# Linear attention and a feed-forward layer on one core: the issue order and the engine choices of the whole program set by another table

## The chip, the cores and the metric

The kernel runs on one core of a Trainium2 chip. The metric is the device time of one execution in microseconds (us), lower is better. Three runs of the kernel before took 789.76, 793.84 and 795.9 us. One further execution was recorded by the profiler; all rows below come from it.

## The reference

Linear attention over `q`, `k`, `v` of 8 batches, 8 heads, 576 positions and head width 64, followed by a feed-forward layer on the 4608 tokens that come out of it:

```python
q_s = softmax(q, axis=-1)                    # over the head width
k_s = softmax(k, axis=2)                     # over the positions
kv = einsum('bhsd,bhse->bhde', k_s, v)
x = einsum('bhsd,bhde->bhse', q_s, kv)       # -> 4608 tokens x 512
h = x @ w_in                                 # 512 x 2048
g = where(h >= 1, h, where(h <= -1, 0, (h + 1)**2 / 4))
out = g @ w_out                              # 2048 x 512
```

All is wanted in float32. `w_in` and `w_out` reach the device in float64, as two 32-bit words per number.

## The kernel before, in words

**Numbers.** A float32 product is made of two rounded parts per operand (high and low, type fp32r) and three matmuls: high by low, high by high, low by high. The high part is a copy with a cast on ScalarE (`high`, L1878), the low part a subtraction on VectorE or GpSimd (`low`, L1881). The weights are joined from their two words on the chip in the same manner (L597 to L639) and written to device memory, from which later stages fetch them (`fetch` L702, `fetch_second` L1861).

**Stages.** The tokens are worked in 9 chunks of 512. For a chunk, the attention of its batch is loaded (L1053 for the first batch, L1299 for the others; `q` tiles of a place share a ring of two buffers), the softmaxes are made, `k` and `q` are transposed (L1348, L1518; `kb`, `ta`, `tb`), TensorE forms `kv` (L1104, L1365), `kv_scaled` (L920 on ScalarE, L922 on VectorE) divides it by the softmax sums into `kvt`, and TensorE forms `x` from `ta`, `tb` and `kvt` (L944) in two PSUM banks that it borrows from earlier products. The first layer gives `h` in 16 blocks of 128 of the 2048 columns, the activation is a rectifier (L1738), a square (L1742 on ScalarE, L1744 on GpSimd) and a min of the two (`g_min`, L1748, VectorE), and the second layer adds up the outputs.

The first 3 chunks run plainly: `h` (L1583) and `o` (L1783), with `g_lo` (L1774) for the low part of an activation. The other 6 chunks run as 3 pairs. A pair's two layers use a form of matrix product with 7 products in place of 8 (P1 to P7): `two_first_layers` sums them in the PSUM banks `hA`, `hC` and `hb` (L1647), with snapshots of a bank (`sn`, L479 on ScalarE, L481 on VectorE) that are added to other banks (L1671); the second layer has the sums `oA` and `oX` (L1893), in two groups of four steps per pair, whose operands are combinations of activations (`change`, L1843). In the names, `hA_3_6` is bank hA of the pair that begins with chunk 3, in the 7th of its 8 steps of two blocks, and `g2_3_0_P7_1` the second operand of product P7 in the first group of that pair. One product is 6 matmuls of 512 columns.

**What sets the order.** The program first lists 3479 operations with their dependencies, without issuing them. Each has one engine or two ways to choose from. `Plan.settle()` then makes one global order of them from two written tables:

```python
for n in SECOND:
    self.ops[n].engine = self.ops[n].ways[1][0]
done = set()
for n in SEQUENCE:
```

`SEQUENCE` holds every operation's number once, `SECOND` those that run on the second of their two engines. The operations are emitted in that order, each into the queue of its engine, and an engine works its queue strictly in order. DMAs are all issued from SyncE (SP) in order, too: one that must wait for a buffer holds those behind it. TensorE (PE) has no second way for any operation. A ring hands its buffers to the operations that take them in the order in which they are listed, whatever the tables say.

Of the kernel before, what the change touches and what calls it, by code (L numbers as in the profile page):

```python
# [114 lines left out]
class Ring:  # L115
# [17 lines left out]
    14, 0, 1, 13, 42, 82, 41, 22, 55, 2, 3, 54, 15, 23, 4, 89, 9, 24, 5, 96, 16, 10, 43, 50, 11,  # L133
    25, 51, 17, 12, 56, 6, 18, 117, 27, 84, 83, 29, 44, 52, 85, 7, 19, 33, 30, 63, 86, 8, 20,
    53, 31, 64, 45, 26, 34, 57, 87, 21, 65, 35, 28, 58, 32, 46, 66, 124, 341, 36, 91, 47, 68,
    90, 48, 70, 59, 37, 92, 39, 49, 38, 74, 60, 40, 71, 97, 321, 61, 93, 75, 98, 67, 62, 72, 99,
    76, 94, 104, 69, 118, 73, 147, 119, 77, 100, 323, 120, 101, 134, 78, 80, 79, 135, 154, 125,
    81, 105, 121, 126, 106, 127, 122, 107, 343, 128, 136, 149, 108, 175, 129, 322, 162, 148,
    109, 137, 150, 182, 163, 110, 151, 324, 164, 111, 152, 155, 165, 112, 138, 156, 113, 205,
    166, 139, 157, 342, 115, 177, 158, 192, 167, 176, 140, 114, 178, 325, 116, 141, 159, 183,  # L140
    193, 326, 179, 212, 184, 194, 142, 180, 195, 185, 327, 168, 146, 196, 233, 328, 143, 207,
    206, 88, 330, 186, 220, 208, 169, 144, 344, 209, 187, 221, 197, 210, 170, 240, 222, 333,
    198, 172, 345, 213, 214, 329, 263, 223, 199, 215, 123, 145, 224, 200, 171, 234, 346, 347,
    216, 250, 235, 225, 251, 217, 236, 331, 252, 226, 237, 332, 174, 270, 227, 238, 253, 334,
    228, 173, 349, 242, 291, 241, 278, 348, 336, 254, 481, 243, 279, 265, 244, 204, 335, 264,
    203, 245, 351, 255, 202, 266, 350, 298, 201, 256, 271, 483, 232, 272, 267, 293, 257, 231,
    273, 268, 352, 229, 274, 258, 292, 280, 275, 360, 294, 281, 353, 308, 367, 282, 300, 354,
    309, 295, 355, 482, 299, 310, 296, 283, 301, 230, 484, 260, 302, 356, 388, 284, 337, 485,
    357, 358, 285, 501, 311, 303, 338, 286, 340, 339, 261, 359, 361, 395, 375, 312, 369, 502,
    362, 376, 313, 486, 363, 262, 390, 368, 314, 377, 364, 370, 378, 315, 365, 316, 289, 379,  # L150
    319, 389, 423, 380, 259, 391, 487, 405, 397, 396, 488, 381, 371, 406, 489, 503, 392, 287,
    398, 382, 372, 407, 504, 408, 383, 430, 418, 393, 505, 409, 506, 451, 507, 438, 394, 419,
    493, 491, 420, 439, 490, 410, 492, 440, 399, 290, 411, 424, 425, 288, 400, 386, 412, 426,
    458, 441, 509, 642, 413, 496, 427, 416, 508, 494, 428, 317, 431, 495, 318, 442, 511, 385,
    644, 510, 520, 432, 468, 443, 181, 433, 320, 512, 452, 387, 453, 434, 444, 469, 435, 454,
    445, 470, 459, 446, 384, 527, 460, 239, 414, 461, 513, 455, 471, 514, 643, 456, 497, 472,
    515, 522, 462, 548, 535, 498, 463, 499, 500, 645, 473, 536, 521, 474, 517, 537, 555, 720,
    523, 415, 529, 524, 447, 516, 475, 525, 417, 518, 421, 476, 448, 528, 662, 477, 530, 583,
    646, 297, 550, 449, 549, 647, 519, 538, 557, 663, 648, 565, 551, 539, 479, 556, 540, 531,
    450, 558, 552, 566, 422, 532, 559, 541, 567, 649, 560, 542, 478, 590, 664, 457, 543, 578,  # L160
    721, 568, 579, 553, 480, 665, 569, 611, 598, 554, 580, 570, 526, 545, 584, 571, 544, 666,
    592, 599, 572, 585, 581, 586, 600, 722, 547, 587, 573, 591, 601, 588, 593, 575, 602, 667,
    546, 594, 582, 603, 621, 650, 595, 622, 604, 623, 668, 605, 740, 624, 723, 606, 724, 574,
    759, 625, 669, 577, 652, 613, 727, 612, 726, 626, 725, 741, 653, 670, 728, 756, 651, 681,
    742, 757, 614, 576, 627, 615, 743, 760, 628, 758, 616, 607, 589, 671, 672, 800, 729, 753,
    673, 654, 608, 629, 730, 754, 674, 655, 630, 761, 731, 656, 766, 762, 732, 631, 675, 683,
    763, 676, 657, 610, 733, 636, 764, 767, 682, 637, 734, 677, 768, 744, 634, 769, 735, 765,
    679, 609, 796, 678, 632, 701, 745, 797, 248, 680, 633, 792, 635, 746, 770, 702, 737, 924,
    801, 793, 747, 779, 684, 780, 640, 781, 685, 771, 802, 795, 736, 755, 772, 153, 782, 803,
    794, 686, 658, 748, 804, 687, 638, 807, 693, 659, 773, 688, 839, 690, 783, 689, 750, 774,  # L170
    784, 738, 694, 703, 751, 833, 806, 805, 808, 660, 785, 809, 704, 840, 836, 820, 834, 691,
    810, 739, 705, 837, 811, 821, 841, 786, 749, 692, 812, 842, 752, 787, 877, 696, 776, 843,
    706, 695, 845, 846, 813, 844, 822, 879, 211, 823, 707, 920, 798, 814, 306, 847, 708, 249,
    709, 815, 848, 799, 824, 661, 925, 775, 921, 916, 711, 777, 710, 917, 849, 926, 790, 923,
# [2099 lines left out]
```

## Time and profile before

| | |
|---|---|
| median of three runs | 793.84 us |
| lowest and highest run | 789.76, 795.9 us |
| the profiled execution: span | 790.7 us |
| TensorE busy | 782.4 us (99%), 4144 matmuls |
| weight loads of TensorE (PEld) | 631.7 us (80%) |
| VectorE (DVE) | 630.8 us (80%), 1067 instructions |
| ScalarE (ACT) | 498.2 us (63%), 1002 instructions |
| GpSimd (POOL) | 382.8 us (48%), 321 instructions |
| DMA queues | 71.8% of 16 engines' time, 193 MB |

Busy is the time in which at least one instruction of the engine ran. The profiled execution has no time of its own beside the span; the span is 3.1 us below the median of the runs, and inside their spread. The granted TensorE clock is full in all 40 slices of the span, and TensorE is shown busy at 90% or more in all slices but the first, which has 80 to 90%.

### The profile page before, as it was taken

What the parts mean: (1) busy time and instruction counts of PE and PEld (TensorE: products, weight loads), DVE (VectorE), ACT (ScalarE), POOL (GpSimd) and SP (SyncE); (2) the same over time, 40 slices, a digit from 0 to 9 for tenths busy, and PEclk for the clock granted to TensorE, in tenths of its full rate; (3) what the DMA queues carried; (4) which work ended last, traced back from release to release, by engine and by line L of the source; (5) the groups of instructions that cost most, each with busy time, mean ns of one, the idle gap of its engine ahead of it and who ended that gap; (6) DMA issues with size and microseconds to landing.
All of it is one profiled execution on the core that took longest, in us unless ns stands there. A gap on an engine that the chain in (4) does not pass through costs nothing.

```text
span 790.7 us, 12342 instructions
## 1 busy us (share of the span) xinstructions
PE 782.4 (99%) x4144; PEld 631.7 (80%) x4144; DVE 630.8 (80%) x1067; ACT 498.2 (63%) x1002; POOL 382.8 (48%) x321
## 2 busy tenths in 40 slices
PE   8999999999999999999999999999999999999998
PEld 7777788878787788877878778787877888888886
DVE  7888999877877898888889998777779755765684
ACT  6888777565776666665676766544657644455452
POOL 4554546664657554275254355545540444541532
PEclk9999999999999999999999999999999999999999
DMA  8787967978896879886766768666567557656572
GB/s 325 228 314 228 327 229 280 356 236 282 256 323 213 272 252 323 264 291 226 242 236 233 256 210 283 225 208 223 190 216 258 204 182 267 196 204 225 177 251 91
DMA packets 72783, 193.79 MB, mean 245 GB/s; under 512 B 8080, under 2 KB 14480, under 8 KB 72720
## 3 DMA queue, kind: packets, MB, share of 16 engines
q1 hardware_dynamic: 72720, 193.00, 71.8%
q8 instruction: 33, 0.54, 0.3%
q14 instruction: 30, 0.25, 0.1%
HBM read 148.93 MB, written 44.04 MB: 244 GB/s over the span
## 4 chain that ended last, share of the span: by engine, by line
PE 91%; DVE 4%; ACT 2%; DMA 1%; issue 1%; POOL 0%; DVEq 0%; SPq 0%; ACTq 0%
PE hA L1647 16%; PE oA L1893 16%; PE h L1583 15%; PE o L1783 14%; PE oX L1893 12%; PE hC L1647 8%; PE hb L1647 4%; PE x L944 2%; PE kv L1365 2%; DMA xw<-in_w 1%; PE warm L2202 1%; PE oA L1905 1%; PE kv L1104 0%; DMA kt<-in_kt 0%; ACT r L1742 0%
## 5 line engine op out<-in xcount | busy, mean ns | idle before, releaser
L1647 PE MATMUL hA<-x,w 128*128 128x512 f32 x576 | 146.2, 391 | 0.6 <-DVE g L1748 0.6
L1893 PE MATMUL oA<-g_P,w_P 128*128 128x512 f32 x558 | 138.2, 391 | 0.0
L1878 ACT CAST g_P<-g 128x512 fp32r<-128x512 f32 x144 | 87.4, 619 | 70.6 <-PE oX L1893 28.9
L1647 PEld LDWEIGHTS hA<-x,w 128*128 128x128 f32 x576 | 107.5, 188 | 24.3 <-DVE g L1748 1.0
L1893 PEld LDWEIGHTS oA<-g_P,w_P 128*128 128x128 f32 x558 | 104.0, 188 | 23.9 <-issue 0.9
L1881 POOL TENSOR_TENSOR g_P<-g,g_P 128x512 fp32r<-128x512 f32 x52 | 70.5, 1359 | 102.3 <-ACT g_P L1878 77.6
L1783 PE MATMUL o<-wh,g 128*128 128x512 f32 x384 | 118.6, 390 | 0.1
L1893 PE MATMUL oX<-g_P,w_P 128*128 128x512 f32 x432 | 106.9, 390 | 0.0
L1893 PEld LDWEIGHTS oX<-g_P,w_P 128*128 128x128 f32 x432 | 80.8, 188 | 17.8 <-ACT g_P L1878 0.6
L1881 DVE TENSOR_TENSOR g_P<-g,g_P 128x512 fp32r<-128x512 f32 x92 | 70.9, 782 | 23.6 <-ACT g_P L1878 23.4
L1783 PEld LDWEIGHTS o<-wh,g 128*128 128x128 f32 x384 | 72.1, 188 | 15.2 <-DVE g L1774 0.5
L1583 PE MATMUL h<-x,w 128*128 128x512 f32 x312 | 81.0, 392 | 0.0
L1783 PE MATMUL o<-wl,g 128*128 128x512 f32 x192 | 75.7, 394 | 0.0
L1744 POOL TENSOR_TENSOR r<-r 128x512 f32<-128x512 f32 x38 | 40.6, 1073 | 68.2 <-ACT r L1738 68.2
L1647 PE MATMUL hC<-x,w 128*128 128x512 f32 x288 | 73.2, 389 | 0.0
L1583 PE MATMUL h<-x,x 128*128 128x512 f32 x264 | 69.0, 392 | 0.7 <-DVE g L1774 0.7
L1583 PEld LDWEIGHTS h<-x,w 128*128 128x128 f32 x312 | 58.0, 188 | 14.5 <-issue 1.6
L1742 ACT ACTIVATE r<-r 128x512 f32<-128x512 f32 x106 | 66.6, 631 | 1.4
L1647 PEld LDWEIGHTS hC<-x,w 128*128 128x128 f32 x288 | 54.0, 188 | 11.4 <-DVE g L1748 0.3
L1583 PEld LDWEIGHTS h<-x,x 128*128 128x128 f32 x264 | 49.2, 188 | 12.3 <-DVE g L1774 1.1
L1783 PEld LDWEIGHTS o<-wl,g 128*128 128x128 f32 x192 | 36.0, 188 | 9.6 <-issue 2.1
L1738 ACT ACTIVATE r<-h,half 128x512 f32<-128x512 f32 x48 | 32.8, 686 | 15.3 <-PE h L1583 14.8
(167 smaller groups left out, 1445.3 us busy)
## 6 DMA issues: line engine op xcount, KB each, us to landing
w_P<-v_P SPq DMA_DIRECT2D x84, 512.0 KB, 4.6
w<-s SPq DMA_DIRECT2D x48, 512.0 KB, 4.9
w<-b SPq DMA_DIRECT2D x40, 512.0 KB, 5.0
v<-in_v SPq DMA_DIRECT2D x32, 325.0 KB, 5.9
q<-in_q SPq DMA_DIRECT2D x36, 256.0 KB, 4.0
k<-in_k SPq DMA_DIRECT2D x28, 320.0 KB, 4.5
st<-in_w SPq DMA_DIRECT2D x16, 512.0 KB, 5.1
xw<-in_w SPq DMA_DIRECT2D x16, 512.0 KB, 5.7
```

Of the source, the lines that this page charges most:

```text
L944: nc.tensor.matmul(t[r][cols, :, p0:p1], kvt[rows, g % NKV, pr, :], q[pr]["tq"][rows, :, p0:p1], start=True, stop=True, tile_position=(r * ...
L1365: nc.tensor.matmul(kv[d, i, :], t[pr]["k"][:, j, d], t[pr]["v"][:, j, e * (D + 1) : (e + 1) * (D + 1)], start=(j == 0), stop=(j == KJ - 1) ...
L1583: nc.tensor.matmul(t["h"], lhs, rhs, start=(turn == 0 and i == 0), stop=(turn == NPAIR - 1 and i == 2),)
L1647: nc.tensor.matmul(banks[b]["h"], lhs, rhs, start=(begins and not kk and not m), stop=(ends and kk == 1 and m == 2), skip_group_check=True,)
L1738: nc.scalar.activation(t["r"], t["h"], AF.Relu, bias=half[:, :1], scale=0.5)
L1742: nc.scalar.activation(t["r"], t["r"], AF.Square)
L1744: nc.gpsimd.tensor_tensor(t["r"], t["r"], t["r"], ALU.mult)
L1783: nc.tensor.matmul(outs[c, j], t["g"][:, k, s], rhs, start=(begins and i == 0), stop=(closes and i == 2),)
L1878: nc.scalar.copy(t["g"][:, 0, :], tile_of(i, b))
L1881: by(engine).tensor_tensor(t["g"][:, 1, :], tile_of(i, b), f32(t["g"][:, 0, :]), ALU.subtract)
L1893: nc.tensor.matmul(banks[side, d], wr[c, group, k, i // 2][:, i % 2, w, d * P : (d + 1) * P], t["g"][:, g, :], start=(begins and w == 1), ...
L1905: nc.tensor.matmul(banks[SIDES[k], d], wr[c, group, k, i // 2][:, i % 2, w, d * P : (d + 1) * P], t["g"][:, g, :], start=False, stop=(ends ...
```

## The change

Only the numbers in `SEQUENCE` and `SECOND` change. The operations, their shapes and their dependencies are the same. 376 operations run on another engine than before: 148 go from POOL to DVE and 109 from DVE to POOL, 45 from DVE to ACT and 40 from ACT to DVE, 22 from POOL to ACT and 12 from ACT to POOL. Counted in instructions as issued, DVE goes from 1066 to 1118, ACT from 996 to 993 and POOL from 315 to 266 (a few operations, such as a copy by quarters, are four instructions). PE has the same 4144 matmuls, of its 767 operations 581 at another place of its queue, by 18 places at most; SP has the same 505 DMAs. The new tables take two more lines, so that every line of the code behind them has a number higher by 2 (L1647 becomes L1649).

```diff
 SEQUENCE = (
-    14, 0, 1, 13, 42, 82, 41, 22, 55, 2, 3, 54, 15, 23, 4, 89, 9, 24, 5, 96, 16, 10, 43, 50, 11,
...
+    0, 14, 1, 13, 42, 41, 82, 54, 55, 3, 2, 15, 4, 89, 22, 43, 333, 5, 23, 96, 56, 117, 9, 24,
...
 SECOND = (
-    7, 23, 32, 35, 73, 94, 139, 159, 167, 187, 347, 348, 380, 393, 400, 428, 499, 508, 516, 540,
...
+    7, 20, 32, 35, 64, 94, 139, 167, 180, 187, 217, 238, 365, 393, 400, 428, 443, 463, 553,
...
```

Number 0 is the load of the first `kt` tile and 14 that of the first `q` tile: the first two DMAs of SP change places.

**PE, first chunk, ahead of the last quarter of `h_0_7`.** The bank of `h_0_7` is freed by the low part of `h_0_5`'s activation, `g2_0_5`, on DVE. Before:

```order
L1583 MATMUL h_0_6_721<-x2_458,w_0_6_696 128x512 x3
L1583 MATMUL h_0_6_721<-x3_460,w_0_6_696 128x512 x3
L1583 MATMUL h_0_7_803<-x0_375,x13_771 128x512 x3
L1583 MATMUL h_0_7_803<-x1_378,x13_771 128x512 x3
L1583 MATMUL h_0_7_803<-x2_458,x13_771 128x512 x3
L1783 MATMUL o_0_1_558<-wl4_105,g2_0_4_705 128x512
```

The change:

```order
L1585 MATMUL h_0_6_736<-x1_382,w_0_6_708 128x512 x3
L1785 MATMUL o_0_3_575<-wl4_105,g2_0_4_698 128x512
L1785 MATMUL o_0_3_575<-wh4_104,g2_0_4_698 128x512 x2
L1585 MATMUL h_0_6_736<-x2_463,w_0_6_708 128x512 x3
L1585 MATMUL h_0_6_736<-x3_471,w_0_6_708 128x512 x3
L1585 MATMUL h_0_7_807<-x0_379,x13_768 128x512 x3
```

In both, `h_0_7` follows the end of `h_0_6`. Its first row comes at the 94th place of the queue before and at the 96th now; counted in products of three matmuls, one more stands ahead of it. On DVE `g2_0_5` goes from the 91st place to the 89th.

**PE, second group of blocks of the first pair, ahead of `x_5_1`.** `x_5_1` takes two banks: one is freed by the second scaling of `kv_6_1` into `kvt`, the other by `g_3_12`, the activation made of `hb_3_6`. Before, from the first product of `hA_3_6` (first row of each product; the row behind the last is `x`):

```order
L1647 MATMUL hA_3_6_4672<-x0_2805,w_3_6_0_4509 128x512 x3
...
L1893 MATMUL oA0_3_0_3973<-g2_3_0_P7_0_4584,w2_3_0_P7_0_4493 128x512 x2
...
L1647 MATMUL hA_3_6_4672<-x8_3415,w_3_6_1_4566 128x512 x3
...
L1893 MATMUL oA0_3_0_3973<-g2_3_0_P7_1_4603,w2_3_0_P7_0_4493 128x512 x2
...
L1647 MATMUL hC_3_6_4736<-x6_3068,w_3_6_1_4566 128x512 x3
...
L1893 MATMUL oA0_3_0_3973<-g2_3_0_P7_2_4632,w2_3_0_P7_1_4638 128x512 x2
...
L1647 MATMUL hC_3_6_4736<-x4_3103,w_3_6_2_4634 128x512 x3
...
L1647 MATMUL hA_3_6_4672<-x10_3505,w_3_6_2_4634 128x512 x3
...
L1893 MATMUL oX0_3_0_4542<-g2_3_0_P3_0_4743,w2_3_0_P3_0_4630 128x512 x2
...
L1893 MATMUL oA0_3_0_3973<-g2_3_0_P7_3_4716,w2_3_0_P7_1_4638 128x512 x2
...
L944 MATMUL x_5_1_0_4825<-ta_5_2_4238,kvt_94 64x4x80
```

The change:

```order
L1649 MATMUL hA_3_6_4673<-x0_2908,w_3_6_0_4541 128x512 x3
...
L1895 MATMUL oX0_3_0_4591<-g2_3_0_P5_3_4619,w2_3_0_P5_1_4476 128x512 x2
...
L1895 MATMUL oA0_3_0_3937<-g2_3_0_P7_0_4668,w2_3_0_P7_0_4537 128x512 x2
...
L1895 MATMUL oA0_3_0_3937<-g2_3_0_P7_1_4701,w2_3_0_P7_0_4537 128x512 x2
...
L1649 MATMUL hC_3_6_4728<-x6_3194,w_3_6_1_4666 128x512 x3
...
L1649 MATMUL hA_3_6_4673<-x8_3387,w_3_6_1_4666 128x512 x3
...
L1649 MATMUL hC_3_6_4728<-x4_3188,w_3_6_2_4695 128x512 x3
...
L946 MATMUL x_5_1_0_4776<-ta_5_2_4316,kvt_94 64x4x80
```

Ten products stood between the start of `hA_3_6` and `x_5_1`; now there are seven. ACT in the same stretch, before:

```order
L1738 ACTIVATE r_3_12_4747<-hb_3_6_4642,half_93 128x512
L479 COPY sn_P5_3_6_4758<-hC_3_6_4736 128x512
L479 COPY sn_P1_3_6_4697<-hA_3_6_4672 128x512
L479 COPY acc220_3_4777<-oX0_3_0_4542 128x512
L1878 CAST g2_3_0_P3_1_4782<-c22_3_1_3907 128x512
```

The change:

```order
L1740 ACTIVATE r_3_12_4726<-hb_3_6_4628,half_93 128x512
L481 COPY acc221_3_4737<-oX1_3_0_4592 128x512
L922 ACTIVATE kvt_94<-kv_6_1_4562,rz_6_1_4609 128x64
L481 COPY sn_P5_3_6_4753<-hC_3_6_4728 128x512
L1880 CAST g2_3_0_P7_3_4756<-g_4_6_4259 128x512
L1744 ACTIVATE r_3_12_4726<-r_3_12_4726 128x512
L481 COPY sn_P1_3_6_4697<-hA_3_6_4673 128x512
```

The scaling of `kv_6_1` was on DVE, 3 rows behind `g_3_12`; now it is on ACT. The square of `r_3_12` was on POOL; now it is the sixth of these rows on ACT, behind the snapshot `sn_P5_3_6` of `hC_3_6`.

**SP and DVE, end of the first pair's first group.** `w2_3_1_P2_0` and `w2_3_1_P1_1` are weights of the second group, `q_8_0` a load of the last batch, whose buffer is that of `q_7_0` and comes free with its transpose `ta_7_0`. SP before:

```order
L1861 DMA w2_3_1_P1_0_4933<-v1_P1_151 128x1024
L1299 DMA v_7_1_4938<-in_v 128x650
L1861 DMA w2_3_1_P1_1_4992<-v1_P1_151 128x1024
L702 DMA w_5_0_0_4996<-b0_112 128x1024
L1861 DMA w2_3_1_P2_0_5027<-v1_P2_152 128x1024
...
L1861 DMA w2_3_1_P5_0_5246<-v1_P5_154 128x1024
L1299 DMA q_8_0_5251<-in_q 128x512
```

The change:

```order
L1863 DMA w2_3_1_P1_0_4930<-v1_P1_151 128x1024
L704 DMA w_5_0_0_4959<-b0_112 128x1024
...
L1301 DMA v_7_1_4964<-in_v 128x650
L1301 DMA q_8_0_5000<-in_q 128x512
L1863 DMA w2_3_1_P2_0_5033<-v1_P2_152 128x1024
L1863 DMA w2_3_1_P1_1_5037<-v1_P1_151 128x1024
L1226 DMA xc_5_1_5085<-xk5_2_162 128x512
```

`q_8_0` stood 13 DMAs behind `w2_3_1_P2_0`; now it stands directly ahead of it and of `w2_3_1_P1_1`. DVE around `ta_7_0`, before:

```order
L1881 TENSOR_TENSOR g2_3_1_P2_2_5135<-g_3_13_4925,g2_3_1_P2_2_5135 128x512
L1881 TENSOR_TENSOR g2_3_1_P1_3_5138<-g_3_14_5018,g2_3_1_P1_3_5138 128x512
L1493 TENSOR_TENSOR q_7_0_4682<-q_7_0_4682,qzb_7_0_4968 128x512
L1518 STREAM_TRANSPOSE tb_7_1_5176<-q_7_1_4729 128x512
L1518 STREAM_TRANSPOSE ta_7_0_5180<-q_7_0_4682 128x512
L1843 TENSOR_TENSOR g_3_11_4714<-g_3_11_4714,g_3_10_4601 128x512
```

The change:

```order
L1673 TENSOR_TENSOR hb_3_7_4937<-hb_3_7_4937,sn_P1_3_7_4900 128x512
L1495 TENSOR_TENSOR q_7_1_4699<-q_7_1_4699,qzb_7_0_4948 128x512
L1495 TENSOR_TENSOR q_7_0_4684<-q_7_0_4684,qzb_7_0_4948 128x512
L1520 STREAM_TRANSPOSE ta_7_0_4993<-q_7_0_4684 128x512
L1883 TENSOR_TENSOR g2_3_1_P1_0_4995<-g_3_8_4392,g2_3_1_P1_0_4995 128x512
L483 COPY sn_P5_3_7_5002<-hC_3_7_4977 128x512
L1951 TENSOR_TENSOR acc120_3_4626<-oX0_3_0_4591,acc120_3_4626 128x512
L1883 TENSOR_TENSOR g2_3_1_P1_1_5011<-g_3_10_4600,g2_3_1_P1_1_5011 128x512
```

`ta_7_0` moved to a place three rows behind the sum `hb_3_7`, and the snapshot `sn_P5_3_7`, which was on ACT, stands on DVE two rows behind it. That snapshot must have read `hC_3_7` before TensorE adds the next product to that bank.

## Rows read from the trace of the kernel before

**Rows 1.** The page: busy us, share, instructions of each engine.

```profile
PE 782.4 (99%) x4144; PEld 631.7 (80%) x4144; DVE 630.8 (80%) x1067; ACT 498.2 (63%) x1002; POOL 382.8 (48%) x321
```

**Rows 2.** Waits of PE: line, engine waited for, us, times, longest.

```profile
PE warm L2202 <- POOL ident masks.py:199: 1.4, 1, 1.4
PE x L944 <- DVE kvt L922: 1.1, 1, 1.1
PE ep L1083 <- ACT kt L1078: 0.8, 1, 0.8
PE h L1583 <- DVE g L1774: 0.7, 1, 0.7
PE hA L1647 <- DVE g L1748: 0.6, 1, 0.6
```

**Rows 3.** Timeline, 426 to 452: start, us, engine, line, operation, out<-in, count.

```profile
428.19 2.88 PE L1893 MATMUL oA<-g_P,w_P 128*128 128x512 f32 x12
```

**Rows 4.** Timeline, the end; [idle before, and what ended it].

```profile
787.04 0.75 DVE L1985 TENSOR_TENSOR acc<-oA,acc 128x256 f32<-128x256 f32 x2 [0.76 <-PE oA L1905]
```

**Rows 5.** Timeline, the start.

```profile
1.18 0.42 SPq L1053 DMA_DIRECT2D kt<-in_kt  x1
...
6.38 1.11 PE L1083 MATMUL ep<-ident,kt 128*128 128x128 f32 x4 [0.81 <-ACT kt L1078]
...
17.23 2.04 POOL L1127 TENSOR_TENSOR q<-q,qz 128x512 f32<-128x512 f32 x2 [2.69 <-DVE k L481]
...
19.33 0.42 PEld L1143 LDWEIGHTS tp<-ident,q 128*128 128x128 f32 x4 [0.23 <-POOL q L1127]
```

**Rows 6.** Timeline, 53 to 56.5, PE.

```profile
52.79 1.52 PE L1583 MATMUL h<-x,w 128*128 128x512 f32 x6
...
55.02 1.66 PE L1583 MATMUL h<-x,x 128*128 128x512 f32 x6 [0.71 <-DVE g L1774]
```

**Rows 7.** Timeline, 408 to 417.5, PE and the scaling of kv_6_1.

```profile
408.57 1.52 PE L1893 MATMUL oA<-g_P,w_P 128*128 128x512 f32 x6
...
410.79 0.27 DVE L922 TENSOR_SCALAR kvt<-kv,rz 128x64 f32<-128x64 f32 x1
...
411.21 0.49 PE L944 MATMUL x<-ta,kvt 64*64 64x320 f32 x2 [1.12 <-DVE kvt L922]
...
413.73 1.52 PE L1647 MATMUL hA<-x,w 128*128 128x512 f32 x6
...
415.81 1.66 PE L1647 MATMUL hA<-x,w 128*128 128x512 f32 x6 [0.55 <-DVE g L1748]
```

**Rows 8.** Timeline, 395 to 411.3: product into hC_3_6 and its snapshot.

```profile
401.77 1.52 PE L1647 MATMUL hC<-x,w 128*128 128x512 f32 x6
...
403.33 0.59 ACT L479 COPY sn_P<-hC 128x512 f32<-128x512 f32 x1 [0.15 <-PE hC L1647]
```

**Rows 9.** The page, costliest groups: busy, mean ns | idle before, and its end.

```profile
L1878 ACT CAST g_P<-g 128x512 fp32r<-128x512 f32 x144 | 87.4, 619 | 70.6 <-PE oX L1893 28.9
...
L1881 POOL TENSOR_TENSOR g_P<-g,g_P 128x512 fp32r<-128x512 f32 x52 | 70.5, 1359 | 102.3 <-ACT g_P L1878 77.6
...
L1881 DVE TENSOR_TENSOR g_P<-g,g_P 128x512 fp32r<-128x512 f32 x92 | 70.9, 782 | 23.6 <-ACT g_P L1878 23.4
```

**Rows 10.** Windows: us, busy PE PEld DVE ACT POOL, PEclk, DMA share, GB/s.

```profile
100.00:120.00 20.00, 20.00 (x90) 16.56 (x89) 19.27 (x35) 14.88 (x32) 9.65 (x9) 1.00 0.68 235
620.00:640.00 20.00, 20.00 (x90) 16.57 (x89) 12.97 (x20) 9.32 (x16) 6.91 (x6) 1.00 0.66 224
```

**Rows 11.** The page, DMA issues: KB each, median us to landing.

```profile
w_P<-v_P SPq DMA_DIRECT2D x84, 512.0 KB, 4.6
```

**Rows 12.** Timeline, 426 to 452: use of the second group's weights, transpose, load.

```profile
438.95 2.88 PE L1893 MATMUL oX<-g_P,w_P 128*128 128x512 f32 x12
...
444.31 0.66 DVE L1518 STREAM_TRANSPOSE ta<-q 128x512 f32<-128x512 f32 x1
...
450.63 0.85 SPq L1299 DMA_DIRECT2D q<-in_q  x2
```

492 rows, old and new, of tables (SECOND, SEQUENCE) are left out of this document.

## Prediction

> **What bounds the kernel now.** I read the page first: TensorE is busy 782.4 of 790.7 us, while VectorE, the next, is at 80% [rows 1]. Then the waits of TensorE, because only there can another order win anything: five are over half a microsecond, and two of them are at the start [rows 2]. Then the timeline around each. TensorE's busy time is taken up step by step: twelve matmuls of 512 columns in a row last 2.88 us and six 1.52 [rows 3, 7], so each further one costs 1.36 / 6 = 0.227 us and a product of six 1.36 us. The work of TensorE is the same 4144 matmuls after the change, so its 782 us stay. The rest of the span is 8.3 us: 1.4 before the first matmul, 0.8 for `ep`, 2.4 in the three later waits [rows 2], and 790.7 − 787.0 = 3.7 after the last matmul, whose result VectorE takes up at 787.04 [rows 4].
>
> **The start.** `kt` now goes ahead of the first `q`. The `ep` transpose waited 0.8 us for the exponential of `kt` [rows 5], so the most it can gain is 0.8. But a chain behind it has no room: POOL's scaling of the last two `q` ends at 17.23 + 2.04 = 19.27, and the transposes that use it start at 19.33, 0.06 later [rows 5]; an earlier `ep` doesn't move that chain, unless its loads move too. I take −0.3, with 0 and −0.8 as ends.
>
> **The three waits.** The wait as printed is idle time; the delay is start minus the end of the step ahead.
> - `h_0_7`: the step ahead began at 52.79 and takes 1.36, `h_0_7` began at 55.02 [rows 6]: 0.87 lost. The change puts one more product of three matmuls ahead of it, 0.68, and moves `g2_0_5` two places up on VectorE: −0.7 to −0.87, I take −0.8.
> - `x_5_1`: 408.57 + 1.36 to 411.21, 1.28 lost behind the scaling of `kv_6_1` on VectorE, which ended at 411.06 [rows 7]. In the change that scaling is early on ScalarE, and `g_3_12` decides. Take T as the start of `hA_3_6`. Seven products put `x_5_1` at T + 9.5. The product into `hC_3_6` is the fifth, so it starts at T + 5.44; before, one that began at 401.77 had its snapshot begun at 403.33, 1.56 later, 0.59 long [rows 8]. ScalarE then has the snapshot (T + 7.0 to 7.6), a cast and the square, about 0.62 each [rows 9], to T + 8.8; `g_3_12` on VectorE, at most 0.78 [rows 9], is done at T + 9.6. That is where `x_5_1` arrives: the wait goes, but nothing is left in hand. −1.2, with 0 (VectorE held up by as much) and −1.28 as ends.
> - `hA_3_7`: 413.73 + 1.36 to 415.81, 0.72 lost for `g_4_12` [rows 7]. In the change `hA_3_7` follows `x` (1.16 with its switch: 411.21 to 413.73, less one product) and three more products, near T + 14.8; the sum into `hC_3_6` can start when its seventh product is done, T + 9.7, and an addition, rectifier, cast, square and min of at most 0.78 each end by T + 13.6. −0.7, ends 0 and −0.72.
>
> Together −2.7, at most −2.87.
>
> **Moved work.** 148 + 40 operations come to VectorE and 109 + 45 leave it, 34 more; by 0.782 each [rows 9] that is 27 us, so VectorE is busy about 658 of 790 us, 83%. POOL gives up 49 operations of about 1.36, some 66 us, and ScalarE takes 15 more of 0.62, 9 us [rows 9]. None of that is on the path by itself: what hides it is TensorE's full queue. Where the cover is thin it costs: from 100 to 120 us VectorE is already busy 19.27 of 20 us, while from 620 to 640 it has 7 us free [rows 10]. So I cost the moves at nothing as a sum, and price the places where VectorE is now late as new waits.
>
> One such place can be worked out. In the change, 33 rows of VectorE lead from `g_3_12` to the snapshot `sn_P5_3_7`, and `hC_3_7`'s next product, which must not overwrite it, stands 17 products and `x` behind `x_5_1`: 17 × 1.36 + 1.16 = 24.3 us. By the mean of all VectorE instructions, 630.8 / 1067 = 0.59 [rows 1], the 33 rows, 36 instructions with a copy by quarters, take 21.3 us, by 0.782 each 25.8 [rows 9]: from 3.0 in hand to 1.5 late. All three old waits were for VectorE, and it gets more work, so I take new waits of 1.0 in all, one or two of the size of the old ones; the ends are 0 and 5.8, twice what the old three cost. Below 0 can't be, since 1.4 + 0.8 + 2.4 + 3.7 is already all of the 8.3 us.
>
> The tail: the last operations of TensorE are the same; 0, with 3.7 staying.
>
> **Sum.** 790.7 − 0.3 − 2.7 + 1.0 = 788.7 for a profiled execution. That execution's span is 3.1 below the median of the runs (its time outside the span isn't shown), so **791.8 us** as a median, 0.3% faster; I call that no change, since less than 1% (7.9 us, below 785.9 or above 801.8) is what runs that spread from 789.8 to 795.9 can't tell apart.
>
> **Rivals.**
> - *Old waits give way to new ones of the same sum.* For it: VectorE at 83%, `x_5_1` without anything in hand, 24.3 us against 21.3 to 25.8. Against: the three long waits are each answered by a visible move. Span 790.7, time 793.8.
> - *All waits go.* 790.7 − 0.8 − 2.87 = 787.0, time 790.1. For it: order changes on TensorE are by 18 places at most, each of a size that a few matmuls give. Against: the two thin places above. Even this is under 1%.
> - *SP is held.* `q_8_0` waits for `ta_7_0`, and the weights of P2 and P1 stand right behind it. Before, that transpose ended at 444.31 + 0.66 = 445.0 and the load went out at 450.63, harming nobody; the first product of P2 began at 438.95 [rows 12]. In the change those products come about where they did. A weight load takes 4.6 us to land [rows 11] and two issues ahead of it some 0.7: if the transpose still ended at 445.0, P2 would start at 450.3 and TensorE would be 450.3 − 438.95 = 11.4 us behind where it was, whatever was won ahead of it: 802.1, time 805.2. The point from which it decides: `ta_7_0` ending later than 438.95 − 5.3 − 2.0 (0.3 + 2.7 − 1.0, what TensorE wins ahead of it) = 431.7. By the order it stands two rows of VectorE ahead of the thin snapshot above, and that snapshot is due four products and `x`, 6.6 us, ahead of P2: at 438.95 − 2.0 − 6.6 = 430.4, so `ta_7_0` ends near 428.8, 2.9 in time, if VectorE is.
> - *TensorE isn't the bound at all.* TensorE at 99% counts matmuls that overlap; weight loads are only 80% busy [rows 1]. In a stretch without a wait the loads are at 16.57 of 20 us, 83% [rows 10], for the same 90 matmuls in a stretch with a crowded and one with an idle VectorE, so 83% is what a full queue looks like. Were the gap free time, the next engine would decide, VectorE at 658, time 661. The Trainium skill, "Perfetto Trace Analysis", section "Identifying the Most-Contended Engine", says that matmul busy time is a bad measure and weight-load busy time a good one; by that rule alone 20% would be open, and the two windows here speak against it.
> - *The tables do nothing that the queues feel:* 793.8, as the first.
>
> **Chances.** Forecast 0.45; same sum 0.25; all waits gone 0.15; SP held 0.10; TensorE not the bound 0.02; nothing felt 0.03. By the ends of its terms the forecast itself spans 790.1 (787.0 + 3.1) to 799.6 (790.7 + 5.8 + 3.1), most of it the new waits. The range 786 to 798 takes in the first three cases with the spread of a median of few runs, and leaves SP held, TensorE not the bound and the forecast's worst end outside; 786 and not 790 at the low end because single runs were up to 4.1 below their own median. Faster by over 1% needs more than every wait there is, 0.07 with an odd median and the fourth rival; slower by over 1% is SP held and a like mishap, 0.11; within 1% 0.82.
>
> **What would show it.** In the profile after: TensorE busy within 2 us of 782 with x4144; VectorE near 658, POOL near 317. Waits of TensorE: `h` for `g`, `x` for `kvt` and `hA` for `g` gone or under 0.3, `ep` below 0.8; in their place one or two new ones on VectorE, of half to one microsecond, first `hC` for a snapshot `sn` on VectorE near 430, or `x` for `g` near 407. If `oX` near 438 waits for a DMA, SP was held. The granted clock stays at 1.00, as it did through all waits here [rows 10]. I am wrong if the waits' sum after the start is over 4 us, or if a wait of several microseconds stands where none was.

## The result and the profile after

The changed kernel takes **801.42 us** in the median of six runs (797.97 to 806.74), the kernel before 793.82 in six beside it (789.76 to 795.9): a ratio of 1.0102 [1.007, 1.0135]. A second set of six gave 1.0107 [1.0083, 1.0132]. I had predicted 791.8, 786 to 798. The change is 1% slower, and the prediction has the wrong sign.

The profiled execution of the change took 802.27 us with a span of 800.5, 9.8 more than the span before. The list of runs shows 1.8 us outside the span, where I had put 3.1 between span and median: the execution profiled before took about 792.5, 1.3 below the median.

The page, as [rows 1, 9, 11], with the busy us, share and count of each engine first:

```profile
PE 784.8 (98%) x4144; PEld 632.4 (79%) x4144; DVE 637.5 (80%) x1119; ACT 504.2 (63%) x999; POOL 320.3 (40%) x272
...
L1883 DVE TENSOR_TENSOR g_P<-g,g_P 128x512 fp32r<-128x512 f32 x102 | 73.2, 725 | 22.6 <-ACT g_P L1880 22.3
...
w_P<-v_P SPq DMA_DIRECT2D x84, 512.0 KB, 5.0
```

TensorE is still the bound, with 2.4 us more busy time; the other 7.4 us of the 9.8 are idle time (790.7 − 782.4 = 8.3 before, 800.5 − 784.8 = 15.7 now). VectorE got 52 instructions more and only 6.7 us more busy time. A weight load of the second layer takes 5.0 us to land, in the median, in place of 4.6. The waits of TensorE, as [rows 2] (us, times, longest):

```profile
PE hA L1649 <- DMA w<-b: 3.6, 1, 3.6
PE h L1585 <- DVE g L1776: 2.9, 2, 1.7
...
PE ep L1085 <- ACT kt L1080: 1.1, 1, 1.1
PE oA L1895 <- DMA w_P<-v_P: 1.0, 1, 1.0
PE hC L1649 <- DMA w<-s: 0.7, 1, 0.7
PE tp L1145 <- POOL q L1129: 0.5, 1, 0.5
PE et L1088 <- DVE tb L483: 0.5, 1, 0.5
PE o L1785 <- DVE g L1776: 0.2, 1, 0.2
```

The three waits of before are gone. In their place stand three for DMAs (5.3 us), where there were none, and three for VectorE (3.1). Both signs by which I had said I would be wrong have come: the waits after the start add up to 8.4 us, over 4, and one of 3.6 stands where none was. To see where each microsecond was lost, I compared the start times of matmuls in the two traces at equal amounts of matmul work. The lag of the change behind before goes in steps:

| place (us of the span) | step | what stands there |
|---|---|---|
| start, to 20 | +0.9 | `q` and its transposes |
| 52 to 57 | −0.6 | the old wait of `h_0_7`, gone |
| 92 | +1.1 | `h` waits for `g` on VectorE |
| 182 | +2.0 | `h` waits for `g` on VectorE |
| 255 to 300 | +0.7 | no single wait |
| 302 to 321 | +6.1 | `hA` waits for a weight load (4.5), then a lower clock (1.6) |
| 353 | +0.9 | `oA` waits for a weight load |
| 414 | +0.8 | `hC` waits for a weight load |
| 412 to 420 | −1.5 to −2.0 | the old waits of `x_5_1` and `hA_3_7`, gone |
| 470 to 500 | −0.55 | small ones |
| end | +9.8 | (steps read at points: they add up to within 0.5) |

**The largest step.** The timeline of the change from 296 to 316 (start, us, engine, line, operation):

```profile
296.84 0.62 ACT L782 CAST w_s<-ss 128x512 fp32r<-128x512 f32 x1
...
299.26 0.69 DVE L1457 TENSOR_REDUCE qa<-q 128x16 f32<-128x512 f32 x1 [1.82 <-DMA q<-in_q]
...
301.06 0.68 DVE L786 TENSOR_TENSOR w_s<-ss,w_s 128x512 fp32r<-128x512 f32 x1
...
301.77 0.32 SPq L830 DMA_DIRECT2D s<-w_s  x1
...
306.06 0.32 SPq L704 DMA_DIRECT2D w<-b  x1
...
313.49 1.99 PE L1649 MATMUL hA<-x,w 128*128 128x512 f32 x6 [3.61 <-DMA w<-b]
```

and the chain of waits there:

```profile
301.77 4.23 DMA s<-w_s
...
306.06 7.38 DMA w<-b
```

`w_s` is a combination of weights; its low part goes to device memory (`s<-w_s`), and a later load (`w<-b`) must wait for that store. Before, POOL made the low part 0.07 us after its cast. Now it is on VectorE behind two reductions that wait for a load of `q`: 3.6 us after the cast ended. The store takes 4.23 to land, the load then 7.38. Before, the load was issued 4.0 us ahead of its matmul:

```profile
299.96 0.32 SPq L702 DMA_DIRECT2D w<-b  x1
...
303.94 1.55 PE L1647 MATMUL hA<-x,w 128*128 128x512 f32 x6
```

In that trace it had landed at 303.72: 0.22 us ahead of its use ("in hand" below), in a profile in which TensorE waits for no DMA at all. That landing of 3.8 us was a quick one. In runs 11, 12 and 15 below, which keep before's loads up to here, the same load takes 5.1 to 6.0, and `hA` waits 0.4 to 1.1 for it; so up to 1.1 of the 6.1 is the luck of the one execution that I predicted from. The windows after the wait (us, busy PE PEld DVE ACT POOL, PEclk, DMA share, GB/s):

```profile
314.00:318.00 4.00, 4.00 (x12) 3.10 (x12) 1.94 (x4) 0.59 (x1) 0.00 (x0) 0.58 0.04 16
318.00:322.00 4.00, 4.00 (x19) 3.32 (x18) 1.83 (x3) 3.84 (x10) 1.69 (x2) 1.00 0.51 134
```

After 3.61 us of idle TensorE, the granted clock is 0.58 for four microseconds, so mostly at the lower of its two levels: 12 matmuls where the next four have 19.

**The step at 182.** The change's timeline from 175 to 185:

```profile
178.79 1.35 DVE L483 COPY kh<-ka 64x8 f32<-64x8 f32 x2
178.82 1.30 POOL L786 TENSOR_TENSOR w_s<-ss,w_s 128x512 fp32r<-128x512 f32 x1 [3.09 <-ACT w_s L782]
...
180.08 1.29 POOL L850 TENSOR_TENSOR vw<-wh,wl 128x512 f32<-128x512 f32 x1
180.18 1.74 DVE L786 TENSOR_TENSOR w_s<-ss,w_s 128x512 fp32r<-128x512 f32 x1
...
183.32 0.68 DVE L1776 TENSOR_TENSOR g<-h,g 128x512 fp32r<-128x512 f32 x1
...
184.05 1.19 PE L1585 MATMUL h<-x,w 128*128 128x512 f32 x4 [1.72 <-DVE g L1776]
```

Two copies of 64x8 take 1.35 us and a subtraction 1.74, each while POOL runs an instruction of 1.3. The activation's low part `g`, for which TensorE waits, stands behind them. In both traces VectorE's instructions last longer beside POOL when all their inputs are in SBUF: the low parts (L1881 before) 0.68 alone, and 1.00 in the mean where POOL runs beside them for over 0.1 us; in the change 0.69 and 0.88. Those with an input in PSUM, the transposes and the reductions last the same. The Trainium skill, "SBUF — State Buffer", section "SBUF: two separate sides", says that VectorE and GpSimd share a pair of ports which one instruction holds to its end, so that the other "fully blocks"; these rows agree.

### The profile page after: what moved, and what is told of

Same layout as the page of the kernel before. It is cut to its first block, busy times and chain, and to the rows that moved or that the text cites. A ratio compares the mean times of both kernels' runs of the same rounds, so it can differ in the third digit from the quotient of the medians.

```text
span 800.5 us, 12278 instructions
## 1 busy us (share of the span) xinstructions
PE 784.8 (98%) x4144; PEld 632.4 (79%) x4144; DVE 637.5 (80%) x1119; ACT 504.2 (63%) x999; POOL 320.3 (40%) x272
## 4 chain that ended last, share of the span: by engine, by line
PE 82%; DVE 6%; DMA 6%; ACT 3%; issue 1%; POOL 0%; SPq 0%; DVEq 0%; ACTq 0%
PE oA L1895 15%; PE hA L1649 15%; PE h L1585 12%; PE oX L1895 12%; PE o L1785 11%; PE hC L1649 8%; PE hb L1649 4%; PE x L946 2%; PE kv L1367 2%; DMA w<-s 1%; DMA w<-b 1%; DMA w_P<-v_P 1%; DMA st<-in_w 1%; DVE g L1776 1%; ACT sg L606 1%
## 5 line engine op out<-in xcount | busy, mean ns | idle before, releaser
L1649 PE MATMUL hA<-x,w 128*128 128x512 f32 x576 | 145.3, 391 | 3.6 <-DMA w<-b 3.6
L1649 PEld LDWEIGHTS hA<-x,w 128*128 128x128 f32 x576 | 107.7, 188 | 26.9 <-DMA w<-b 4.0
L1883 POOL TENSOR_TENSOR g_P<-g,g_P 128x512 fp32r<-128x512 f32 x42 | 54.9, 1311 | 142.4 <-ACT g_P L1880 126.4
L1883 DVE TENSOR_TENSOR g_P<-g,g_P 128x512 fp32r<-128x512 f32 x102 | 73.2, 725 | 22.6 <-ACT g_P L1880 22.3
L1649 PE MATMUL hC<-x,w 128*128 128x512 f32 x288 | 73.3, 390 | 0.7 <-DMA w<-s 0.7
L1744 ACT ACTIVATE r<-r 128x512 f32<-128x512 f32 x116 | 72.6, 630 | 1.6
L1649 PEld LDWEIGHTS hC<-x,w 128*128 128x128 f32 x288 | 53.9, 188 | 12.3 <-ACT r L1744 1.1
L1746 POOL TENSOR_TENSOR r<-r 128x512 f32<-128x512 f32 x28 | 31.0, 1112 | 64.9 <-ACT r L1740 61.5
L1341 POOL TENSOR_TENSOR k<-k,kc 128x640 f32<-128x640 f32 x19 | 25.5, 1345 | 49.7 <-DVE kc L1333 46.9
```

The lines of the kernel that those rows point to most:

```text
L1341: by(engine).tensor_tensor(k, k, at, ALU.subtract)
L1649: nc.tensor.matmul(banks[b]["h"], lhs, rhs, start=(begins and not kk and not m), stop=(ends and kk == 1 and m == 2), skip_group_check=True,)
L1744: nc.scalar.activation(t["r"], t["r"], AF.Square)
L1746: nc.gpsimd.tensor_tensor(t["r"], t["r"], t["r"], ALU.mult)
L1883: by(engine).tensor_tensor(t["g"][:, 1, :], tile_of(i, b), f32(t["g"][:, 0, :]), ALU.subtract)
```

## The experiments

Experiments write their tables in the lines of the table before, so their line numbers are those of before (L1583, L1647). The diffs are schematic: numbers are operations. Ratios are to the kernel before, run beside it.

**1 and 2: which part of the program loses.** The change's first 1056 operations (to 200 us of TensorE) and then before's order, and the reverse with before's first 1077:

```diff
-SEQUENCE = after
+SEQUENCE = after[:1056] + [n for n in before if n not in after[:1056]]
```

> The order and the engines of the change for all that it issues up to the point where TensorE is at 200 us, the rest in the order and on the engines of before. Theory L (most of the loss is loads that reach their use with too little lead, the worst at 309 us of the changed kernel) expects what stands ahead of 200 us in the two profiles: TensorE is 3.7 us later there (0.9 at the start, 1.1 at 92, 2.0 at 182, minus 0.6 at 55), so 3 to 4.5 us over before, 797 to 798. Theory V (it is VectorE and POOL, wherever they are crowded) expects the same here. A theory that the loss is spread evenly over the program expects a quarter of 8, 2 us.

> The reverse: before up to 200 us, the change's order and engines behind it. By the two profiles TensorE loses 6.0 more us after 200 (6.1 around 309, 0.9 at 353, 0.9 at 414, minus 2.0 for the two old waits near 412 and 0.5 later): 4 to 7 us over before, 798 to 801, if theory L is right, since the thin loads are all behind 200 us; and a wait of several us of hA for a load near 305. If the wait at 309 was an accident of one execution, it is 0 to 1 us over before.

Measured: 799.93 us, 1.0084 [1.0069, 1.01], and 803.38, 1.0129 [1.0092, 1.0167]. The first keeps the steps of the change's beginning (+0.8 and, at 182, +2.0), the second lacks them; but both lose at the joint near 210, 3.8 and 5 to 7 us, where loads and casts that one order had done are still to do in the other. So a splice adds its own waits, and the halves can't be added up. What the two runs show is that the loss is in more than one place.

**3 and 4: the queue of SP alone.** SP's DMAs in before's order with all else from the change, and the reverse:

```diff
-SP's operations at their places in after
+SP's operations at the places, counted in TensorE's operations, that they have in before
```

> The changed kernel with its DMAs (all of SP's queue) put back to where they stood among TensorE's operations before, as far as their inputs allow; TensorE, VectorE, ScalarE and POOL keep the order and the engines of the change. Theory L expects the waits of TensorE for DMA (3.6, 1.0 and 0.7 us) to go and the leads of the weight loads to come back (about 20 of 196 under 3 us, where the change has 55): 5 to 7 us below the changed kernel, 794 to 796. Theory V expects no gain, 800 to 802.

> The kernel before with only SP's queue changed: each DMA where the change puts it among TensorE's operations, as far as its inputs allow; all engines' order and choices as before. Theory L expects thin leads (40 or more of 196 weight loads under 3 us) and waits of TensorE for DMA of 2 to 6 us in sum, 796 to 800. Theory V expects 793 to 795.

Measured: 842.01, 1.0621 [1.0586, 1.0655], and 847.12, 1.0668 [1.064, 1.0696]. Both are far off what I expected. TensorE's waits are then mostly for VectorE and ScalarE, which wait 64 and 67 us for DMAs (6.5 before, 28.6 in the change): in each table the order of the loads is fitted to the order of the engines, and breaking that fit costs some 50 us. That doesn't decide between the theories; it says that no queue can be judged by itself.

**5: fewer of POOL's instructions beside VectorE.** The three operations of POOL at 92 and 182 to VectorE:

```diff
 SECOND = (
+    525, 1083, 1091,
```

> The changed kernel with three operations put from POOL to VectorE, in the same order: the weight subtraction that POOL begins at 91.0 us, and the two at 178.8 and 180.1. Theory V (in the two new waits of h for g, at 92 and 182 us, VectorE is held while POOL runs on the same SBUF operands: a conversion takes 1.45 in place of 0.42, a small copy 1.35 in place of 0.33, a subtraction 1.74 in place of 0.68) expects the two waits to shrink although VectorE gets three more subtractions of 0.68: the wait at 182 from 1.7 to about 1.0, and the three long VectorE instructions to be gone; the time 0 to 1.5 below the changed kernel. The rival (VectorE simply has too much to do there) expects both waits 0.7 to 1.4 longer, and the time 1 to 2 above.

Measured: 800.74, 1.0092 [1.0075, 1.0109]. Its timeline from 176 to 190:

```profile
177.38 0.35 DVE L481 COPY kh<-ka 64x8 f32<-64x8 f32 x2
...
177.75 0.69 DVE L784 TENSOR_TENSOR w_s<-ss,w_s 128x512 fp32r<-128x512 f32 x1
...
179.24 0.68 DVE L784 TENSOR_TENSOR w_s<-ss,w_s 128x512 fp32r<-128x512 f32 x1
179.84 1.29 DVE L848 TENSOR_TENSOR vw<-wh,wl 128x512 f32<-128x512 f32 x2
...
181.04 0.68 DVE L1774 TENSOR_TENSOR g<-h,g 128x512 fp32r<-128x512 f32 x1
...
181.78 1.65 PE L1583 MATMUL h<-x,w 128*128 128x512 f32 x6 [0.63 <-DVE g L1774]
```

VectorE has two instructions more there, and is done sooner: the copies take 0.35 in place of 1.35, `w_s` 0.68 in place of 1.74, and the wait is 0.63 in place of 1.72. The steps fall from 1.1 to under 0.1 and from 2.0 to 0.9. At 182 POOL's hold on VectorE is the cause; at 92 the step comes and goes in the change itself, and run 13 shows when. The total hardly shows it: the loads further on still come late (`hA` waits 3.0 us).

**6 to 8: repairing the loads by hand.** Number 6 puts the one low part of the largest step back on POOL, right behind its cast; 7 moves 37 weight loads that had under 3 us in hand up by 1 to 18 places in SP's queue (its diff is such moves alone); 8 does both and lists operation 476 ahead of 529 and 978 ahead of 1086.

```diff
 SECOND = (
-    1560,
 SEQUENCE = (
-    1658, ..., 1560, ..., 1561,
+    1560, 1561, 1658, ...,
```

> The changed kernel with one operation given back to POOL, the low part of the last sum of first-layer weights (on VectorE it stands behind two reductions that wait for a q load until 299 us), and with the store that needs it ahead of one load in SP's queue. The store's landing is what the weight load of hA at 309 us waits for before it may be issued. Theory L: that load goes out about 1.5 to 3 us earlier, the wait of hA for DMA falls from 3.6 to 0 to 1.5 us, and TensorE's clock isn't lowered behind it: 3 to 6 us below the changed kernel, 795.5 to 798.5. If the long wait was the accident of a slow landing (7.4 us), the wait stays or is gone without any of this and the time is within 1 us of 801.4.

> The changed kernel with only 37 of SP's 505 DMAs moved up in its queue, by 1 to 18 places: weight loads whose room was free over 1 us before they were issued and that landed under 3 us ahead of use. Theory L expects the waits of TensorE for DMA behind 330 us (1.0 and 0.7) to go and the loads with under 3 us in hand to fall from 55 of 196 to 25 or fewer, while the wait at 309, which isn't among them, stays: 1 to 2.5 us below the changed kernel, 799 to 800.5, and runs that spread less than its 798 to 807. Theory V expects 801 to 802.

> The changed kernel with all of it: the operation given back to POOL with its store ahead, the 37 loads up, and the low part of g ahead of the conversion at 92 us and ahead of the subtraction at 180 us in VectorE's queue. If the steps by which TensorE falls behind in the changed kernel are additive, 6.1 at 309, 0.9 at 353, 0.9 at 414, 1.1 at 92 and 2.0 at 182 go, 11 of them in all, and it comes out at 790 to 793, level with before or up to 0.5% faster (the three old waits of before are then gone too). If the changed order only trades one wait for another, 796 or more.

Measured: 802.26, 1.0119 [1.01, 1.0138]; 804.88, 1.0139 [1.0116, 1.0161]; 801.08, 1.0107 [1.0087, 1.0127]. None is better than the change. In 6 the wait for the load is gone, and another of the same size stands at the same place (waits from 290 to 314):

```profile
ACT x L1251 <- DMA xc<-xk: 4.8, 1, 4.8
...
PE o L1783 <- ACT g L1771: 3.6, 1, 3.6
```

By the chain, that load of `xc` takes 8.27 us to land. In 7 the wait near 309 stays, as I had expected, since its load isn't one of the 37; SP issues the same DMAs around it, and it takes 8.25 us to land. The waits at 353 and 414 are gone, also as expected, but one of 1.6 stands at 622, and the time is no better:

```profile
PE hA L1647 <- DMA w<-b: 4.5, 1, 4.5
...
PE oA L1893 <- DMA w_P<-v_P: 1.6, 1, 1.6
```

The weight loads that land under 3 us ahead of TensorE's first use fall from 55 to 22 in 7, which is what I had asked of it, and to 20 in 8; before it was 18. Neither is faster than the change. So the loss isn't one late operation, and it isn't in the number of thin weight loads either: near 309 whichever load is waited for lands late, and with the weights moved up VectorE and ScalarE still wait 30.8 us (7) and 40.9 us (8) for DMAs.

**9 and 10: half the bytes.** The 196 weight loads (112 for the first layer, 84 for the second) each fetch half. These kernels leave out the low parts of the fetched weights; the high part stands in their place:

```diff
-nc.sync.dma_start(f32(ws_tile(name)[:, :n]), src[:, part])
+nc.sync.dma_start(f32(ws_tile(name, 1)[:, :n]), src[:, part, :1])
...
-nc.sync.dma_start(f32(w2_tile(name)), second[group, k][:, part])
+nc.sync.dma_start(f32(w2_tile(name)), second[group, k][:, part, :1])
```

> The kernel before with every fetched weight block (196 loads of 512 KB) loaded by half, the high part alone, which then stands for the low part too: 50 MB of 194 MB less to move, every other operation, order and engine as before. All theories expect no more than 1 us of difference to before, 792.5 to 794.5, since before shows hardly a wait for DMA on TensorE's path. It is the yardstick for the next run.

> The changed kernel with the same 196 loads by half. Theory L, in the form that it has by now (the change's order lets DMAs arrive just in time or late, for VectorE and ScalarE as much as for TensorE: 33.9 us of waits for DMA on these engines against 6.5 before, in the same places where TensorE falls behind) expects most of the loss to go with the traffic: 791 to 795, at most 1.5 above the same kernel of before, and the waits for DMA down to under 15 us. Theory V (VectorE and POOL, whatever the loads do) expects 798 to 801, as without.

Measured: before 791.11, 0.9999 [0.9986, 1.0012]; the change 795.26, 1.0045 [1.0028, 1.0063]. The page and the waits of TensorE of the change with half loads:

```profile
w_P<-v_P SPq DMA_DIRECT2D x84, 256.0 KB, 3.2
```

```profile
PE h L1583 <- DVE g L1774: 3.7, 4, 2.0
PE warm L2202 <- POOL ident masks.py:199: 1.4, 1, 1.4
PE ep L1083 <- ACT kt L1078: 1.2, 1, 1.2
PE tp L1143 <- POOL q L1127: 0.9, 1, 0.9
PE et L1086 <- DVE tb L481: 0.5, 1, 0.5
PE x L944 <- DVE kvt L922: 0.2, 1, 0.2
```

Loads that land in 3.2 us in place of 5.0 give the kernel before nothing and the change 0.6 of its 1.0 to 1.07 points. No wait of TensorE for a DMA is left, and no step at 302 to 353; the steps at 92 (+1.2) and 182 (+2.2) stay, as do the gains (−2.0 at 410, −0.55 at 500). This tells the two causes apart. It doesn't take away all that I had expected of it: the change is still 4.15 us above its yardstick, where I had said at most 1.5, and TensorE, VectorE and ScalarE still wait 20.4 us for DMAs, where I had said under 15 (33.9 with whole loads, 6.5 before).

**11 and 12: the gains by themselves.** The kernel before, with only the moves that free the old waits: numbers 1940 and 2088 (both waits near 412), and in the first of the two also 230 (that of `h_0_7`).

```diff
 SEQUENCE = (
-    308, ..., 230, ..., 2095, ..., 1940, ..., 1943, ..., 2088,
+    230, 308, ..., 1940, 2095, ..., 2088, 1943, ...,
```

> The kernel before with three operations moved by one place each: one product of the second layer ahead of h_0_7 at 55 us, one product of P3 ahead of x_5_1 at 410 us, and g_4_12 ahead of one low part in VectorE's queue at 413 us. No DMA moves and no engine changes. If the three old waits are each ended by what the prediction named, TensorE gains 0.7, 1.3 and 0.7 us: 790.5 to 791.5, ratio 0.9965. If the waits move on to the next operation, 793 to 794.

> The kernel before with only the two moves at 410 us: the product of P3 ahead of x_5_1, and g_4_12 ahead of the low part in VectorE's queue; nothing moves ahead of 400 us. With all three moves TensorE had won 2.0 us there, and lost what it had won at 55 us and more to kv's transposes and to a weight load at 305 us. If gains stay where no thin load lies behind them: 2.0 us, 790 to 792 or a ratio of 0.9975. If any gain here is taken back later: 0.9995 or more.

Measured: 791.55, 0.9995 [0.9981, 1.0009], and 792.48, 1.0005 [0.9991, 1.002]. No gain that can be told from none, and both intervals leave out the ratios that I had expected, 0.9965 and 0.9975. With all three, 2.0 us are won at 412 to 419, and waits that were not there before take 1.4 and 1.1:

```profile
PE kv L1365 <- DVE st L612: 1.4, 1, 1.4
PE hA L1647 <- DMA w<-b: 1.1, 1, 1.1
```

The wait of `hA` isn't the moves' alone: it is 0.5 in 12 and 0.4 in 15, where nothing is moved ahead of it. With the two, 1.6 us are won and given back by 430.

**13: the change once more.**

> The changed kernel once more, to see which of its steps come back in another execution. Theory L expects the total again near 801, the wait of hA or of what stands next to it at 300 to 310 us again, of a size that differs by 1 us or more, and the steps at 182 and 353 us again within 0.5. If the long wait at 309 was an accident, this profile shows none of it and a time under 797.

Measured: 799.12, 1.0107 [1.0083, 1.0132]. Its waits for loads are other ones:

```profile
PE h L1585 <- DVE g L1776: 1.7, 1, 1.7
...
PE x L946 <- DVE kvt L924: 1.1, 1, 1.1
PE hC L1649 <- DMA w<-s: 1.0, 1, 1.0
...
PE hA L1649 <- DMA w<-b: 0.6, 1, 0.6
```

The 3.6 us at 309 are 0.6 here, and the clock stays at 1.00 through 305 to 320; the step at 182 is +2.0 again, those of 258 to 328 add up to +4.0, and the end is at +6.0. The step at 92 is absent. There the change's first trace has (from 88 to 96)

```profile
91.00 1.31 POOL L641 TENSOR_TENSOR w<-xw,w 128x512 fp32r<-128x512 f32 x1
91.15 1.45 DVE L611 TENSOR_SCALAR st<-st 128x512 uint32<-128x512 uint32 x1
```

and this one (from 87 to 95)

```profile
90.28 0.40 DVE L611 TENSOR_SCALAR st<-st 128x512 uint32<-128x512 uint32 x1
90.36 1.49 POOL L641 TENSOR_TENSOR w<-xw,w 128x512 fp32r<-128x512 f32 x1
```

Where POOL began 0.15 us ahead, VectorE's conversion took 1.45; where VectorE began 0.08 ahead, it took 0.40. The largest row of one profile is one throw of the dice; what lasts is the step at 182, and that the loads have little in hand (54 of 196 under 3 us again).

**14: both causes taken away.** Half loads and the three operations of number 5.

```diff
 SECOND = (
+    525, 1083, 1091,
...
+nc.sync.dma_start(f32(ws_tile(name, 1)[:, :n]), src[:, part, :1])
```

> The changed kernel with loads by half (795.3, 0.45% over before) and with the same three operations put from POOL to VectorE as in an earlier run. If what is left of the loss with loads by half is the holding of VectorE by POOL at 92 and 182 us, the steps there fall from 1.2 and 2.2 us to 0.3 and 1.1, and the time to 793 to 794, 0.2% over before. If VectorE is just too busy, the steps grow by 0.7 and 1.4 and the time to 797.

Measured: 794.12, 1.0018 [1.0009, 1.0027]. That is another 0.27 points off 1.0045, with intervals that only just part. In its profile the step at 92 is +0.3, as expected, and the one at 182 +1.6, where I had expected 1.1. 0.18 points, some 1.4 us, are left.

**15: before first, then the change.** The first 1988 of the 3479 operations in before's order, the others in the change's, so that the thin stretch from 90 to 353 is left out and the gains at 412 are kept.

```diff
-SEQUENCE = after
+SEQUENCE = before[:1988] + [n for n in after if n not in before[:1988]]
```

> Before's order and engines up to its operation 1988 of 3479, somewhat ahead of 400 us, where the two orders have issued all but four of the same operations; the change's order and engines behind it. All profiles of the changed kernel show TensorE winning 2.0 us around 410 and 0.5 at 470, and losing nothing over 0.5 behind 400 but for loads that come late. If the gain at 410 needs the change's order behind it (taken alone it was given back within 20 us), and the joint costs nothing: ratio 0.997, 790. If the change's thin loads behind 400 us or the joint cost as much: 1.000.

Measured: 796.47, 1.0038 [1.0018, 1.0058]. The joint at 392 costs about 3.4 us (2.5 of it in one wait of `hb` for `g`); the gains from 412 to 500 are there, 1.7 to 2.5, and 1.4 more is lost at 606 to 612. No order that I ran beats the kernel before.

## Why the prediction was wrong, step by step

- **TensorE is the bound:** right. It is x4144 and busy 784.8, a little over my 782 ± 2, since one stretch ran at the lower clock. The weight loads are busy only 79%, and still the waits of TensorE lengthen the time, so that share is no measure of free time here.
- **The three waits, −2.7:** right, by the working, in the change's trace: −0.6 at 55 (−0.8), and −1.5 to −2.0 for the other two (−1.9). In the change's timeline from 416 to 426 neither `x` nor `hA` has an idle time ahead of it, against 1.12 and 0.55 [rows 7]:

```profile
416.98 0.77 PE L946 MATMUL x<-ta,kvt 64*64 64x320 f32 x2
...
421.15 4.24 PE L1649 MATMUL hA<-x,w 128*128 128x512 f32 x18
```

- **SP held by `q_8_0`:** right that it wasn't: `oX` waits for no DMA, and the snapshot `sn_P5_3_7` held nobody.
- **The start, −0.3:** wrong sign, +0.9. `ep` did start earlier, but the chain that I had named as the one without room came 0.9 later [rows 5]:

```profile
17.74 0.25 DVE L1197 RECIPROCAL qz<-qz 128x16 f32<-128x16 f32 x1
...
18.13 2.05 POOL L1129 TENSOR_TENSOR q<-q,qz 128x512 f32<-128x512 f32 x2 [3.57 <-DVE k L483]
```

  I had taken that chain as unmoved, while VectorE's order ahead of it changed. The step is larger than this pair of traces shows. The scaling ends at 17.7 to 19.3 us in the six traces that begin in before's order (before, 2, 9, 11, 12, 15), of which the one that I predicted from is the latest, and at 19.6 to 20.7 in the nine that begin in the change's (the change, 1, 5 to 8, 10, 13, 14): 1.6 later in the mean.
- **The new waits, +1.0 with ends 0 and 5.8:** the step that failed. They came to about 11.6 us in the profile, twice the upper end, of which 7.8 at loads (1.6 of it the lower clock behind the longest wait), 3.1 at VectorE beside POOL, and 0.7 that I can't place. I looked for places where VectorE is late, and put the loads at nothing without a reason, but for one place, around `q_8_0`. Had I put every weight load's landing beside TensorE's first use of it, I would have seen a danger: of the 196, 4 landed under 1 us ahead of that use before, and 12 in the change; under 3 us, 18 and 55. From issue to first use the 10th percentile fell from 8.5 to 6.7 us for first-layer loads and from 7.9 to 6.3 for second-layer ones, against landings of weights that reach 8.3 us. The second figures are from the trace after, but the places of SP's loads against TensorE's products were in the two orders before the run, for all 196 and not only for the two behind `q_8_0`. This count is a sign and not the cause: run 7 brought it back to 22 and was no faster. What halving the bytes shows is that the time loads take to land carries most of the loss; which loads, those of weights or those of `q`, `k` and `xc` for which VectorE and ScalarE wait, no run took apart.
- **VectorE's load, 658 us:** 637.5. I priced 34 operations more at 0.782 each. With POOL's busy time down by 62.5 us, VectorE is held less: its low parts take 0.725 in the mean and not 0.782, and what all its instructions last beyond the median of their form falls from 42.1 to 28.5 us in sum. So the mean got better while two places, where POOL and VectorE meet ahead of a `g` that TensorE needs, got worse by 3.1 us.
- **The clock stays at 1.00:** wrong in the profiled execution, where the fall cost 1.6 us; right in the one of run 13.
- **Rival "old waits give way to new ones of the same sum":** the nearest. New waits did take the place of the old, but it looked for them at VectorE alone, which has 3.1 of the 11.6 us, and its size is wrong by a factor of four.

What is shown: the bytes of the loads carry 0.6 of the 1.0 to 1.07 points (9 and 10), POOL's three instructions about 0.27 with the loads out of the way (14 against 10), and alone they can't be told from nothing in the total (5). Open is the last 0.18, some 1.4 us: the start, 1.6 us later by the traces, is of that size, 255 to 300 (+0.7 to +2.1) shows another loss, and no run took them apart.

## What to carry to other kernels

An order judged by the durations of one trace is judged only as far as those durations hold; where a load lands 0.22 us ahead of its use, the next landing of 7 us in place of 4 is time that is lost. So when a change reorders queues, put issue, landing and first use of every load side by side, before and after, for the engines that feed the busiest one as much as for it; a page on which it waits for no DMA says nothing of that. The count of thin weight loads was a sign that misled (run 7). What went along with the time in these runs is the sum of the waits of VectorE and ScalarE for DMAs: 6.2 to 8.6 us in the kernels level with before, 16 to 20 in those 0.2 to 1.3% above it (1, 2, 10, 14, 15), 26 to 41 in the change and in 5 to 8, 64 and 67 in 3 and 4. That is no proof of a cause. And a wait freed at one place is a gain only if the next thin place has room for it: here 1.6 us won at 412 to 419 were given back by 430.

## What the runs showed of the hardware that I had not expected

- The same load of 512 KB landed in 3.8 us in the trace before (299.96 to 303.72), in 5.1 to 6.0 in runs 11, 12 and 15, and in 7.4 (306.06 to 313.45) and 4.5 in the two of the change; a load of `xc` took 8.27 in run 6. With half the bytes in the weight loads the median of the second layer's is 3.2 in place of 5.0.
- Two copies of 64x8 on VectorE take 0.35 us, and 1.35 beside a POOL instruction of 1.30: with two instructions more VectorE went through that place in 4.3 us (177.38 to 181.72) in place of 5.2 (178.79 to 184.00).
- After 3.61 us without a matmul the granted clock was 0.58 for the next four microseconds. The length of the wait alone doesn't tell: with one of 1.98 us that ended at 209.8 in run 1 the clock was 0.50 from 210.8 to 214.2, and with one of 2.52 that ended at 395.3 in run 15 it was 1.00 from 395 to 399.
